# Layer norm of block 1 from the column copy of x, in a kernel of attention and a gated feed-forward

## The chip, the cores and the metric

The kernel runs on one core of a Trainium2 chip. The core has a matrix engine (TensorE, PE in the profile; PEld is its loading of weights), a vector engine (VectorE, DVE), a scalar engine (ScalarE, ACT), GpSimd (POOL) and SyncE (SP), which here only issues transfers. Each engine works off its own list of instructions in order. They meet through semaphores. Transfers between DRAM and the on-chip memory (SBUF) run on 16 DMA engines; SyncE, ScalarE and GpSimd each have a queue of them. Products come out in PSUM, a small memory of eight banks.

The metric is the device time of one execution in microseconds (us), as the median of several runs.

## What is computed

With x of 2048 rows and 512 columns, the reference is, cut to what matters:

```python
xn = _layernorm(x, axis=-1)          # (x - mean) / sqrt(var + 1e-5), row by row
s = _A_ref(xn, A_wqkv, A_wo)         # 32 heads of 16: softmax(q k^T / 4) v, then @ wo
g = _silu(_B_ref(xn, ...))           # (silu(xn @ w_gate) * (xn @ w_up)) @ w_down
return x + s * g
```

All inputs and the output are float32.

## The kernel before

**Blocks and slots.** The 2048 rows of x are four blocks of 512 (`TB`), each of four tiles of 128 rows. A prologue makes queries, keys and values of all blocks. For each block it makes twelve products: eight feature tiles (128 features of q or k by 512 rows) and four value tiles (128 rows by 512 values). Block 0 begins with its value tiles, the others end with them. The loop at the end of the prologue numbers these twelve by `n`; `12 * b + n` is called a slot here. After the prologue the attention and the feed-forward network run interleaved on TensorE; the change does not touch that part.

**Operands in two parts.** Products run in a reduced float32 format, and every operand is split in a high part and the remainder: x into `xt` (hi and lo, two sets, so that block b uses set b % 2), the weights into `wh` and `wl` (features) and `vh` and `vl` (values). A product over 512 inputs is 12 matrix instructions: for each of the four chunks c of 128 inputs hi by wh, lo by wh, hi by wl. So x must be normalised and lie transposed, inputs on partitions.

**Weights.** Twelve pieces of the weights are loaded on SyncE's queue some five slots ahead (`load_w`), cast on ScalarE two slots ahead (`high_w`), and subtracted on GpSimd (`low_w`, which needs the cast). Pieces 8 to 11 are the value weights, 0 to 7 the features in slots 4 to 11; "weight 4" is piece 4, used in slot 8.

**Two ways to a transposed x.** Blocks 0 and 1 load rows. VectorE makes mean and variance of each tile (`stats`), the rate 1 / sqrt(var + eps) of all (`rates`), and the normalised rows (`norm`); TensorE turns them in four 128 by 128 transposes per tile (`turn`), ScalarE copies the high part out of PSUM and VectorE subtracts the low part (`split_x`). Blocks 2 and 3 (`columns_of`) load rows only for the statistics and, beside them, x transposed from a second copy of the input (`A_x_columns`). Mean and rate of each row are then wanted along the free axis on all partitions. So `spread_mr` transposes the eight columns of means and rates on TensorE, copies them on ScalarE into `rows_mr`, and writes them to DRAM (`mr_d`, 4 KB) on ScalarE's queue. `load_mr` reads them back, broadcast to 128 partitions (`wide_mr`, 512 KB). Per chunk of columns VectorE then subtracts and multiplies in place, ScalarE casts the high part, VectorE makes the low part.

**The order.** It is written out by hand. `columns_of` puts its steps into a table by slot: `ats` gives, in this order, the slots of the rows' load, the columns' load, the first statistics, the rates, the spread (its read-back one slot later), and the first chunk, and then, for each chunk, how many slots after the first chunk's slot its low part is made. `step(at, 0, ...)` runs ahead of that slot's product, `step(at, 1, ...)` behind it. Block 1's own steps stand in the loop: `load_x(1)` at n = 2, statistics at 2 and 3, rates at 4, `norm` at 6 to 9, `turn_x` at 7 to 10. Its normalised x goes to DRAM for the feed-forward network (`store_x`, GpSimd's queue); block 0's is copied on chip by ScalarE, one piece per slot (`copy_fx`).

**What limits a slot.** A product's bank is one of four (`pps`). ScalarE squares it and casts it into `parts`, VectorE subtracts, and SyncE stores `parts` (512 KB) to `q_d` or `k_d`; there are four `parts` buffers. The load of block 0 and of each later block's rows goes into `xin`, which is the tile `facc`, or into `raw_x`.

## Time and profile before

| | |
|---|---|
| median of 3 runs | 1385.1 us (1385.07 to 1385.13) |
| the profiled execution | 1385.12 us |
| its span | 1383.3 us, 27675 instructions |
| granted TensorE clock | 1.00 of full speed |

The profile shows one execution. A row of a timeline is: start in us from the span's start, duration in us (of the whole group, where several instructions are merged), engine, line of the kernel, operation, what it writes and reads, shapes, how many; in brackets how long the engine had been idle and what ended that. ACTq and SPq are the issues of transfers. Matrix instructions overlap, so their starts tell the pace better than their durations. In a row of stretches each engine's busy time stands with the number of its instructions in brackets. In the list of waits a row gives who waited for whom, the total, how often, and the longest.

### The profile page before, as it was taken

The numbers are of one execution on the slowest core, as the hardware profiler recorded it, in microseconds if no ns is written. First come the engines' busy times: TensorE is split into PE (matmuls) and PEld (weight loads), VectorE is DVE, ScalarE is ACT, GpSimd is POOL, SyncE is SP. The second block draws the span as 40 slices with busy tenths as digits, with TensorE's granted clock in tenths as the row PEclk, the third lists the DMA queues.
The fourth block names the chain that finished last, engine by engine and source line by source line (L and its number), as shares of the span: only waits on it lengthen the run. The fifth ranks groups of instructions, "written<-read, shape, count | busy, mean of one in ns | idle before, by whom it ended". The sixth has DMA issues, their size and how long they took to land.

```text
span 1383.3 us, 27675 instructions
## 1 busy us (share of the span) xinstructions
PE 1377.5 (100%) x11167; PEld 868.4 (63%) x11167; DVE 775.9 (56%) x1250; ACT 1158.2 (84%) x1943; POOL 103.5 (7%) x145
## 2 busy tenths in 40 slices
PE   9999999999999999999999999999999999999998
PEld 7787666656655665565566555566566556655665
DVE  6655466365545663565465643655466545655656
ACT  6644589888888898899998988888888888899875
POOL 4200100000010000000110000000100000000142
PEclk9999999999999999999999999999999999999999
DMA  7989541134553511233724402356333312234752
GB/s 238 307 283 297 147 106 44 36 77 106 111 128 82 135 44 36 51 90 86 173 56 115 110 13 51 74 127 145 83 78 83 101 25 59 59 86 133 226 188 84
DMA packets 132260, 154.71 MB, mean 112 GB/s; under 512 B 13489, under 2 KB 83137, under 8 KB 131358
## 3 DMA queue, kind: packets, MB, share of 16 engines
q1 hardware_dynamic: 124782, 128.03, 36.1%
q0 software_dynamic: 6880, 24.32, 5.2%
q8 instruction: 89, 1.46, 0.5%
q10 hardware_dynamic: 464, 0.53, 0.1%
q14 instruction: 45, 0.37, 0.1%
HBM read 110.61 MB, written 40.12 MB: 109 GB/s over the span
## 4 chain that ended last, share of the span: by engine, by line
PE 89%; DVE 0%; DVEq 0%; issue 0%
PE acc L450 33%; PE bankx L244 29%; PE score L981 10%; PE single L981 8%; PE banky L244 7%; PE spare L981 1%; PE spare L1036 0%; PE banky L1036 0%; DVE y L1043 0%; PE score L1036 0%; PE single L1036 0%; DVE y L1049 0%; DVEq L1096 0%
## 5 line engine op out<-in xcount | busy, mean ns | idle before, releaser
L450 PE MATMUL acc<-pr,vst 128*17 128x512 f32 x4096 | 459.3, 593 | 0.0
L991 ACT ACTIVATE pr<-single 128x512 f32<-128x512 f32 x762 | 429.3, 604 | 17.2 <-PE single L981 0.5
L984 ACT ACTIVATE pr<-score 128x1024 f32<-128x1024 f32 x318 | 327.9, 1031 | 87.1 <-PE score L981 84.3
L450 PEld LDWEIGHTS acc<-pr,vst 128*17 128x17 f32 x4096 | 115.6, 97 | 279.5 <-issue 275.3
L244 PE MATMUL banky<-fx,guh 64*128 64x512 f32 x896 | 290.8, 392 | 0.0
L244 PE MATMUL bankx<-fx,guh 64*128 64x512 f32 x896 | 290.5, 391 | 0.1
L988 DVE COPY pr<-spare 128x512 f32<-128x512 f32 x194 | 134.1, 691 | 182.5 <-PE spare L981 169.6
L981 PE MATMUL score<-qst,kst 50*128 50x512 f32 x830 | 218.8, 418 | 0.0
L981 PE MATMUL single<-qst,kst 50*128 50x512 f32 x922 | 212.6, 398 | 0.0
L244 PE MATMUL banky<-wd,hh 64*128 64x512 f32 x672 | 196.0, 391 | 0.0
L244 PE MATMUL bankx<-wd,hh 64*128 64x512 f32 x672 | 195.9, 391 | 0.0
L1001 ACT ACTIVATE pr<-pr 128x512 f32<-128x512 f32 x354 | 193.3, 641 | 0.0
L244 PEld LDWEIGHTS bankx<-fx,guh 64*128 64x128 f32 x896 | 166.8, 186 | 21.4 <-DVE guh L205 0.6
L244 PE MATMUL bankx<-fx,gul 64*128 64x512 f32 x448 | 175.6, 392 | 0.0
L244 PE MATMUL banky<-fx,gul 64*128 64x512 f32 x448 | 175.5, 392 | 0.0
L981 PEld LDWEIGHTS score<-qst,kst 50*128 50x128 f32 x830 | 98.9, 184 | 112.9 <-ACT pr L991 69.2
L244 PEld LDWEIGHTS banky<-fx,guh 64*128 64x128 f32 x896 | 166.9, 186 | 1.1
L991 ACT ACTIVATE pr<-score 128x512 f32<-128x512 f32 x194 | 116.9, 603 | 35.5 <-PE spare L981 27.7
L988 DVE COPY pr<-single 128x512 f32<-128x512 f32 x160 | 110.5, 691 | 59.1 <-PE single L981 49.3
L244 PEld LDWEIGHTS bankx<-wd,hh 64*128 64x128 f32 x672 | 125.1, 186 | 17.8
L981 PEld LDWEIGHTS single<-qst,kst 50*128 50x128 f32 x922 | 114.8, 184 | 23.0 <-ACT pr L991 7.6
L244 PEld LDWEIGHTS banky<-wd,hh 64*128 64x128 f32 x672 | 125.1, 186 | 5.9
(191 smaller groups left out, 1689.9 us busy)
## 6 DMA issues: line engine op xcount, KB each, us to landing
gur<-in_B_w_gate_dram SPq DMA_DIRECT2D x56, 256.0 KB
gur<-in_B_w_up_dram SPq DMA_DIRECT2D x56, 256.0 KB
wdr<-in_B_w_down_dram SPq DMA_DIRECT2D x56, 256.0 KB
kst<-k_d SPq DMA_DIRECT2D x192, 64.0 KB
qst<-q_d SPq DMA_DIRECT2D x192, 64.0 KB
fx<-xt_d SPq DMA_DIRECT2D x24, 512.0 KB
q_d<-parts SPq DMA_DIRECT2D x16, 512.0 KB
k_d<-parts SPq DMA_DIRECT2D x16, 512.0 KB
```

The source lines that it names most:

```text
L244: mm(bank, lhs[h], rhs[h], start=start, stop=stop)
L450: mm(acc[h * 32:h * 32 + DH + 1], v[:, kt % CT, h * (DH + 1):(h + 1) * (DH + 1)], probs[2 * i + h // 2][:, h % 2], start=kt == 0, stop=kt ...
L981: mm(banked[h], k[r, j, kc * P:(kc + 1) * P], q[r, j], start=True, stop=True)
L984: exps.append(act(pr, both_banks, AF.Exp, scale=0.25))
L988: dve.tensor_copy(pr[:, h], banked[h])
L991: exps.append(act(pr[:, h], banked[h], AF.Exp, scale=0.25))
L1001: exps.append(act(part, part, AF.Exp, scale=0.25))
```

## The change

Block 1 now goes through `columns_of` too. Its call is `columns_of(1, raw_x, xin, (1, 2, 2, 3, 5, 7, (1, 1, 2, 3)))`: rows into `raw_x` at slot 1, columns into `xin` at slot 2, statistics at 2 and 3, rates behind slot 3's product, the spread ahead of slot 5's, the read-back behind the same product and on GpSimd's queue, the first chunk at slot 7 and one more per slot. The row loads, norms and transposes of block 1 go. The rates run before the first of block 0's copies for the feed-forward network, and those copies move one slot later. Block 2's rows are loaded at slot 9 instead of 7 and its columns at 14 instead of 12; its statistics move from 10 to 12, its rates from 12 to 14, its spread from 14 to 16, while its first chunk stays at 19. Block 3's rows move from 11 to 13 and its statistics from 15 to 17.

```diff
-        def load_x(b):
-            for t in range(NT):
-                load_tile(b * NT + t)
...
         def turn_x(b, t, between=None):
             split_x(b, t, turn(t), between)
-            if t == NT - 1 and b:
-                store_x(b)
...
         def load_mr(b):
-            sp.dma_start(wide_mr, mr_d[b].rearrange("s t p -> s (t p)")[None].to_broadcast([P, 2, TB]))
+            (pool if b == 1 else sp).dma_start(wide_mr, mr_d[b].rearrange("s t p -> s (t p)")[None].to_broadcast([P, 2, TB]))
...
-            step(rated, 0, rates_x)
+            step(rated, b == 1, rates_x)
             step(spread, 0, spread_mr, b)
-            step(spread + 1, 0, load_mr, b)
+            step(*((spread, 1) if b == 1 else (spread + 1, 0)), load_mr, b)
...
-        columns_of(2, raw_x, raw_x, (7, 12, 10, 12, 14, 19, (1, 2, 3, 3)))
-        columns_of(3, xin, raw_x, (11, 24, 15, 24, 26, 31, (1, 2, 3, 3)))
+        columns_of(1, raw_x, xin, (1, 2, 2, 3, 5, 7, (1, 1, 2, 3)))
+        columns_of(2, raw_x, raw_x, (9, 14, 12, 14, 16, 19, (1, 2, 3, 3)))
+        columns_of(3, xin, raw_x, (13, 24, 17, 24, 26, 31, (1, 2, 3, 3)))
...
-                if not b and n == 2:
-                    load_x(1)
...
-                if not b and 6 <= n < 10:
-                    norm(n - 6)
...
-                if b < 2 and 0 <= 12 * b + n - 3 < 16:
-                    copy_fx(12 * b + n - 3)
+                if b < 2 and 0 <= 12 * b + n - 4 < 16:
+                    copy_fx(12 * b + n - 4)
...
-                if not b:
-                    for t in range(NT):
-                        if n == 2 + t // 2:
-                            stats(t)
-                    if n == 4:
-                        rates(0, NT)
-                    if 7 <= n < 11:
-                        turn_x(1, n - 7)
```

Three places show how the instructions move. The first is GpSimd's list from the low part of weight 2 to the store of block 1's x. Before:

```order
L578 TENSOR_TENSOR wl<-wraw,wh 128x512 [waits DMAHW3_49,Activation_49]
L578 TENSOR_TENSOR wl<-wraw,wh 128x512 [waits DMAHW4_49,Activation_49]
L578 TENSOR_TENSOR wl<-wraw,wh 128x512 [waits DMAHW1_49,Activation_49]
L578 TENSOR_TENSOR wl<-wraw,wh 128x512 [waits DMAHW2_49,Activation_49]
L578 TENSOR_TENSOR wl<-wraw,wh 128x512 [waits DMAHW4_49,Activation_49]
L578 TENSOR_TENSOR wl<-wraw,wh 128x512 [waits DMAHW6_49,Activation_49]
L664 DMA xt_d<-xt_171 128x2048 [waits Activation_49]
```

After, the same stretch:

```order
L574 TENSOR_TENSOR wl<-wraw,wh 128x512 [waits DMAHW3_49,Activation_49]
L574 TENSOR_TENSOR wl<-wraw,wh 128x512 [waits DMAHW5_49,Activation_49]
L679 DMA wide_mr<-mr_d 128x1024 [waits DMAHW2_49]
L574 TENSOR_TENSOR wl<-wraw,wh 128x512 [waits DMAHW7_49,Activation_49]
L574 TENSOR_TENSOR wl<-wraw,wh 128x512 [waits DMAHW0_49,Activation_49]
L574 TENSOR_TENSOR wl<-wraw,wh 128x512 [waits DMAHW3_49,Activation_49]
L574 TENSOR_TENSOR wl<-wraw,wh 128x512 [waits DMAHW5_49,Activation_49]
L658 DMA xt_d<-xt_171 128x2048 [waits Activation_49]
```

The read of the broadcast rates stands between the low parts of weights 3 and 4 and waits for the write of `mr_d`.

The second is VectorE's list from slot 5's eviction to just behind slot 9's (`parts` is an eviction; `xt_172` is the low part of block 1's x). Before:

```order
L772 TENSOR_TENSOR parts<-ps,parts 128x512 [waits Activation_49]
L638 TENSOR_SCALAR xn<-facc,mv,mr 128x512 [waits DVE_49]
L772 TENSOR_TENSOR parts<-ps,parts 128x512 [waits Activation_49]
L638 TENSOR_SCALAR xn<-facc,mv,mr 128x512
L772 TENSOR_TENSOR parts<-ps,parts 128x512 [waits Activation_49]
L655 TENSOR_TENSOR xt_172<-acc,xt_171 128x4x128 [waits Activation_49]
L638 TENSOR_SCALAR xn<-facc,mv,mr 128x512 [waits DVE_49]
L772 TENSOR_TENSOR parts<-ps,parts 128x512 [waits DMAHW3_49,Activation_49]
L655 TENSOR_TENSOR xt_172<-extra,xt_171 128x4x128 [waits Activation_49]
L638 TENSOR_SCALAR xn<-facc,mv,mr 128x512 [waits DVE_49]
L772 TENSOR_TENSOR parts<-ps,parts 128x512 [waits DMAHW5_49,Activation_49]
L655 TENSOR_TENSOR xt_172<-acc,xt_171 128x4x128 [waits Activation_49]
```

After, from the evictions of slots 4, 5 and 6, which follow one another, to slot 9's:

```order
L766 TENSOR_TENSOR parts<-ps,parts 128x512 [waits Activation_49] x3
L667 TENSOR_TENSOR facc<-facc,wide_mr 128x512 [waits DMAHW6_49,DMASW2_49]
L667 TENSOR_TENSOR facc<-facc,wide_mr 128x512 [waits DVE_49]
L766 TENSOR_TENSOR parts<-ps,parts 128x512 [waits Activation_49]
L667 TENSOR_TENSOR facc<-facc,wide_mr 128x512
L667 TENSOR_TENSOR facc<-facc,wide_mr 128x512 [waits DVE_49]
L766 TENSOR_TENSOR parts<-ps,parts 128x512 [waits DMAHW1_49,Activation_49]
L667 TENSOR_TENSOR xt_172<-facc,xt_171 128x512
L667 TENSOR_TENSOR xt_172<-facc,xt_171 128x512 [waits Activation_49]
L667 TENSOR_TENSOR facc<-facc,wide_mr 128x512
L667 TENSOR_TENSOR facc<-facc,wide_mr 128x512 [waits DVE_49]
L766 TENSOR_TENSOR parts<-ps,parts 128x512 [waits DMAHW4_49,Activation_49]
```

Where a norm and a low part stood between two evictions, two operations on columns and a low part stand now, and the first of them waits for the read on GpSimd's queue (DMASW2).

The third is ScalarE's list from slot 4's eviction to slot 5's (`top` is the square, `fx` the copy for the feed-forward network). Before:

```order
L770 ACTIVATE top_156<-ps 128x512 [waits PE_49]
L771 CAST parts<-ps 128x512
L811 COPY fx<-xt_169 64x2x512
L624 ACTIVATE nw<-mv,root 128x4 [waits DVE_49]
L574 CAST wh<-wraw 128x512 [waits DMAHW4_49]
L770 ACTIVATE top_157<-ps 128x512 [waits PE_49]
```

After:

```order
L764 ACTIVATE top_156<-ps 128x512 [waits PE_49]
L765 CAST parts<-ps 128x512
L805 COPY fx<-xt_169 64x2x512 [waits Activation_49]
L570 CAST wh<-wraw 128x512 [waits DMAHW5_49]
L675 COPY busy<-extra 8x128 [waits DMASW0_49,PE_49]
L676 DMA mr_d<-busy 8x128 [waits Activation_49]
L764 ACTIVATE top_157<-ps 128x512 [waits PE_49]
```

The square root for the rates has left this place (it runs ahead of weight 2's cast), and the copy and the write of the rates (`busy` is `rows_mr`) stand behind the cast of weight 3.

## The prediction

> **What bounds the kernel now.** I read the page's head, then the chain of work that ended last, then the timeline of the first 80 us engine by engine, because the change touches nothing later.

> ```profile
> span 1383.3 us, 27675 instructions
> ...
> PE 1377.5 (100%) x11167; PEld 868.4 (63%) x11167; DVE 775.9 (56%) x1250; ACT 1158.2 (84%) x1943; POOL 103.5 (7%) x145
> ...
> PE 89%; DVE 0%; DVEq 0%; issue 0%
> ```

> TensorE is busy for 1377.5 of 1383.3 us, and the chain is TensorE's own order and almost nothing else. So work taken off TensorE in the first 45 us shortens the span by its issue time, and a wait put on TensorE there lengthens it by as much. All other engines count only where TensorE comes to wait for them.

> I call the twelve products of a block slots: 0 to 3 are block 0's value tiles, 4 to 11 its feature tiles, 12 the first tile of block 1, 24 the first of block 2.

> ```profile
> 31.81 0.60 PE L643 MATMUL acc<-ident,xn 128*128 128x128 f32 x4
> 32.16 0.70 PE L718 MATMUL ps<-xt,wh 128*128 128x512 f32 x2
> 32.70 0.40 PE L718 MATMUL ps<-xt,wl 128*128 128x512 f32 x1
> 32.94 0.63 PE L718 MATMUL ps<-xt,wh 128*128 128x512 f32 x2
> 33.40 0.39 PE L718 MATMUL ps<-xt,wl 128*128 128x512 f32 x1
> 33.63 0.63 PE L718 MATMUL ps<-xt,wh 128*128 128x512 f32 x2
> ...
> 44.71 1.00 PE L718 MATMUL ps<-xt,wh 128*128 128x512 f32 x2
> 45.55 0.39 PE L718 MATMUL ps<-xt,wl 128*128 128x512 f32 x1
> ...
> 50.68 0.27 PE L680 MATMUL extra<-ident,mr 128*8 128x128 f32 x1
> 50.71 0.71 PE L718 MATMUL ps<-xt,wh 128*128 128x512 f32 x2
> 51.25 0.40 PE L718 MATMUL ps<-xt,wl 128*128 128x512 f32 x1
> ```

> Starts are what counts. Three products take 33.63 - 32.94 = 0.69 us, a slot of twelve 2.8, and a pair 0.46. From 31.81 to 32.70 four transposes and a pair take 0.89, so four transposes cost 0.43.

> **What leaves TensorE's path.** Slots 8 to 11 each lose four transposes: 4 x 0.43 = 1.72. At 44.71 the pair takes 0.84 instead of 0.46: TensorE waits 0.38 for the last tile of block 1, which was turned only at the end of slot 11. That wait goes if the columns are ready in time. Added is one transpose of the rates at slot 5: 51.25 - 50.68 = 0.57 for it and a pair, so 0.11. Together 1.72 + 0.38 - 0.11 = 1.99, about 2.0 us. This is the most that the change can bring, and block 1 would begin at 44.71 - 1.72 + 0.11 = 43.1.

> The removed VectorE and ScalarE work (four norms, four copies and subtractions out of PSUM, four statistics) and the added (four subtractions, four multiplications, four low parts, four casts) lie beside TensorE. They cost nothing as long as block 1's twelve operands stand when TensorE reads them. The later place of the feed-forward copies (one slot) costs nothing either: they fill the same ScalarE time in each slot. The rows and columns are 2 MB on SyncE's queue ahead of weights 4 and 5, where 1 MB of rows stood. The transfers pause just behind them, as the first row below shows, so they have room for the extra 1 MB, and weight 3 is cast only at 25.71, 4 and 5 after it. I take zero there.

> ```profile
> 19.00:23.00 4.00, 4.00 (x19) 3.23 (x18) 3.71 (x9) 2.68 (x5) 2.27 (x3) 1.00 0.03 6
> 26.00:31.00 5.00, 5.00 (x23) 4.05 (x22) 3.40 (x10) 4.84 (x8) 2.60 (x2) 1.00 0.99 286
> 53.00:59.00 6.00, 6.00 (x28) 4.81 (x27) 2.58 (x7) 2.79 (x6) 0.00 (x0) 1.00 1.05 346
> 86.00:91.00 5.00, 5.00 (x23) 4.04 (x22) 1.79 (x4) 1.81 (x4) 0.00 (x0) 1.00 1.02 388
> ```

> These are stretches by engine; the last three columns are granted clock, DMA share and GB/s. The transfers are idle from 19 to 23 us (0.03) and full from 26 to 31 (0.99).

> **The new wait: rates out to DRAM and back.** Before, block 1's mean and rate were used where they were made. Now they go through a transpose, a ScalarE copy, a write (mr_d), and a broadcast read (wide_mr, 512 KB) before VectorE can start. In the new order ScalarE's copy stands behind the cast of weight 3.

> ```profile
> 25.51 0.30 ACT L624 ACTIVATE nw<-mv,root 128x4 f32<-128x4 f32 x1
> 25.71 0.61 ACT L574 CAST wh<-wraw 128x512 fp32r<-128x512 f32 x1
> ...
> 52.93 0.25 ACT L681 COPY busy<-extra 8x128 f32<-8x128 f32 x1
> 53.21 0.52 ACTq L682 DMA_DIRECT2D mr_d<-busy  x1
> ...
> 59.11 0.33 SPq L685 DMA_DIRECT2D wide_mr<-mr_d  x1
> ...
> 85.88 0.27 ACTq L682 DMA_DIRECT2D mr_d<-busy  x1
> ...
> 90.92 0.33 SPq L685 DMA_DIRECT2D wide_mr<-mr_d  x1
> ...
> SPq L685 <- DMA mr_d<-busy: 2.2, 1, 2.2
> ...
> 142.45 0.35 SPq L882 DMA_DIRECT2D s_d<-shift  x1
> ...
> 145.83 0.56 POOL L885 DMA_DIRECT2D sh_d<-s_d  x1 [31.31 <-DMA s_d<-shift]
> ```

> The square root moves away from 25.51, so the cast runs there, the copy from about 26.0, and the write starts at about 26.3. How long this write takes at that place no row shows. Blocks 2 and 3 wrote 4 KB from 53.21 to 59.1 (5.9 us; SyncE waited for it) and from 85.88 to 90.9 at most (5.0), both with full transfers; the small write at 142.45 took 3.4 at a slacker time. At 26.3 the transfers are full, but only for about three microseconds, since 23. I take 4.4, between the slack row and the nearer of the full ones: landed at 30.7, with ends 29.7 and 32.2.

> GpSimd waits for it in its own queue, and behind it stands the low part of weight 4, which slot 8 reads at about 32.4 (31.81 + 0.11 and a pair). With the landing at 30.7, 0.56 for the issue and 1.30 for the low part (both in rows here), it is done at 32.6: late by 0.2, which the later wait swallows.

> The read is priced by what GpSimd's queue moved.

> ```profile
> v_d<-vt POOLq DMA_DIRECT2D x1, 1088.0 KB, 5.3
> sh_d<-busy POOLq DMA_DIRECT2D x1, 256.0 KB, 4.3
> ...
> xt_d<-xt POOLq DMA_DIRECT2D x4, 1024.0 KB, 11.4
> ...
> g_d<-y POOLq DMA_DIRECT2D x16, 256.0 KB, 2.7
> ```

> Last column: us from issue to landing. The first two are of the first 30 us and bracket 512 KB: 4.6. The ends are 4.3 and half of the crowded 11.4, 5.7. So VectorE can begin at W = 30.7 + 0.1 + 4.6 = 35.4, between 34.0 and 38.0. It is done with slot 6's eviction some 2 us after that slot's end at 29.1, so it stands there from about 31.

> [...]

> **What follows from W.** VectorE then works off block 1's columns between the evictions of slots 7 to 10.

> ```profile
> 71.88 1.41 DVE L673 TENSOR_TENSOR raw_x<-raw_x,wide_mr 128x512 f32<-128x512 f32 x2
> 73.21 0.68 DVE L772 TENSOR_TENSOR parts<-ps,parts 128x512 fp32r<-128x512 f32 x1
> 73.81 0.41 DVE L776 TENSOR_TENSOR top<-top,sq 128x512 bf16<-128x512 bf16 x1
> ...
> 79.34 1.46 DVE L673 TENSOR_TENSOR xt<-raw_x,xt 128x512 fp32r<-128x512 f32 x2
> ...
> 78.78 0.63 PE L718 MATMUL ps<-xt,wh 128*128 128x512 f32 x2
> ...
> 26.92 0.80 DVE L633 SCALAR_TENSOR_TENSOR mr<-nw,mr 128x4 f32<-128x4 f32 x1
> ...
> 48.88 0.16 DVE L633 SCALAR_TENSOR_TENSOR mr<-nw,mr 128x4 f32<-128x4 f32 x1
> ...
> 26.40 1.30 POOL L578 TENSOR_TENSOR wl<-wraw,wh 128x512 fp32r<-128x512 f32 x1 [2.17 <-ACT wh L574]
> ```

> Block 2's same chain ran from 71.88 to 80.80, 8.9 us with one eviction in it. Block 1's has four; three more at 0.60 (73.81 - 73.21) make 10.7. Then GpSimd: the four-element operation with two SBUF inputs took 0.80 instead of 0.16 and ended with GpSimd's low part (26.40 + 1.30 = 27.70). So VectorE operations with two SBUF inputs seem to be held while GpSimd runs one. The low parts of weights 6 and 7 fall into the chain; I take 0.8 for each, between nothing and 1.3. That gives 12.3, ends 10.7 and 13.3. ScalarE, which waits for the first column inside its own order and then has an eviction, a copy of 1.05 and a cast in each slot, would come to about the same.

> So the last low part stands at W + 12.3 = 47.7. TensorE needs it for the eleventh product of block 1, at 43.1 + 10 x 2.8 / 12 = 45.4. It waits 2.3 in all, part of it already in slots 10 and 11, where the cast of weights 6 and 7 stands behind ScalarE's wait. The sum is -2.0 + 2.3 = +0.3. In general the change is W - 35.1 for the middle chain, and never below -2.0.

> **Block 2** loses spare time too: its rates now leave at slot 16 and are needed at slot 19, three slots instead of five. In the rows above its last low part ends at 80.80 and is needed at 78.78 + 2.33 = 81.1, so 0.3 to spare. By the same ScalarE order the write leaves at about 58 and the read at about 63 on SyncE, some 4 us later than now (59.11). VectorE may start at 72.2 at the latest, so the read has 9 us. Before it had 12.8 and showed no wait. By the GpSimd rows 512 KB needs 4.3 to 5.7; I take no wait, end +2.5 if it needs all it may have used now.

> The profiled execution took 1385.12 (1383.3 of span and 1.8 around it), the median 1385.1. The sum against the first is 1385.12 + 0.3 = 1385.4.

> **The rivals.**
> - The gain stays whole. It needs W below 33.1. For it speaks the 256 KB row with 2.7: a write of 2.7 and a read of 2.7 + 0.8 for the further 256 KB (at about 320 GB/s) give W = 32.6. Against it stand the full transfers from 26 to 31. Time 1385.1 - 2.0 = 1383.1. [...]
> - The round trip is as slow as block 2's. The write takes 5.9 and the read 5.7: W = 38.0, and the change is +2.9, to +3.9 with the full hold by GpSimd. Weight 4's low part is then at 32.2 + 0.1 + 0.56 + 1.30 = 34.2, and slot 8 already stands for 1.8 of it. Slower begins to be told from W = 37.9. Time 1388.0 to 1389.0.
> - Block 2's read is late behind the stores and loads on SyncE's queue, as worked out: with no loss in block 1 besides the sum, +0.3 + 2.5, 1387.9.
> - The rates don't reach the transposition at slot 5 in time, since VectorE's two-input operation falls beside weight 2's low part. At most 0.6, and it only moves part of the later wait forward. It decides nothing.

> **How the numbers follow.** A change of under 0.2%, 2.8 us, is about what a measurement of this kernel tells from none. The forecast (W between 34 and 37.9, change -1 to +2.7) has 0.50; the whole gain 0.20; the slow round trip 0.17; block 2's late read 0.08; something beyond 2.8 us of gain, say less crowding later, 0.05. The first two are both within 0.2%: 0.70. Slower: 0.17 + 0.08 = 0.25. The range reaches from the whole gain to the slow round trip, 1383.0 to 1388.9, and leaves out its far end and the gain that I cannot name.

> **What would show it.** Right: VectorE idle before its first column operation until 34 to 38 us, with a transfer as releaser; ScalarE idle before the first cast of a column; TensorE late by about 2 us between slots 10 and 12; from there all as before, shifted by less than 1 us. Wrong: a first column operation at about 31 (then -2), or waits of TensorE over 1 us before block 2 or in slot 8.

## The result and the profile after

| | before | after |
|---|---|---|
| median, lowest to highest (6 runs each) | 1385.11 us (1384.84 to 1385.18) | 1392.16 us (1390.94 to 1392.93) |
| the profiled execution | 1385.12 us | 1392.93 us |
| its span, mean granted clock | 1383.3 us, 1.000 | 1391.1 us, 0.997 |

The ratio is 1.005, with a 95% interval of 1.0039 to 1.0061. The kernel is slower by 7.05 us in the median and by 7.8 us in the profiled executions. The forecast was 1385.4 and the range ended at 1388.9, so both are missed.

These rows of the page of the kernel after answer to those shown of before: the span, the engines' busy time, the transfers of code (pieces, MB, share), and the scores' matrix instructions (busy us, mean ns, idle before and its releaser). The last row is from the list of transfers: the broadcast read on GpSimd's queue.

```profile
span 1391.1 us, 27653 instructions
PE 1379.8 (99%) x11152; PEld 869.8 (63%) x11152; DVE 778.6 (56%) x1255; ACT 1157.6 (83%) x1944; POOL 104.5 (8%) x146
q8 instruction: 90, 1.47, 0.5%
L964 PE MATMUL score<-qst,kst 50*128 50x512 f32 x830 | 219.1, 418 | 2.2 <-issue 2.2
wide_mr<-mr_d POOLq DMA_DIRECT2D x1, 512.0 KB, 6.1
```

The page of before has for code and scores:

```profile
q8 instruction: 89, 1.46, 0.5%
L981 PE MATMUL score<-qst,kst 50*128 50x512 f32 x830 | 218.8, 418 | 0.0
```

TensorE has 15 matrix instructions fewer and still 2.3 us more busy time, which points to a lower clock somewhere; the rest of the 7.8 are waits. To place them, take the start of each slot's first product in both profiles, and count from the start of slot 4 (20.61 in before, 20.50 in after), so that the few tenths in which the beginnings differ drop out:

| shift against before, us | slot 12 | slot 14 | slot 24 | slot 25 | slot 47 | end of the span |
|---|---|---|---|---|---|---|
| after | +2.94 | +2.51 | +2.47 | +3.90 | +4.00 | +7.9 |

Three losses stand out: one before slot 12, one at slot 24, and 3.9 us somewhere behind the prologue, in the part that the change does not touch.

**The first loss, at block 1.** The timeline of after, from the transposition of the rates in slot 5 to the first product of block 1:

```profile
23.92 0.27 PE L674 MATMUL extra<-ident,mr 128*8 128x128 f32 x1 [0.46 <-DVE mr L629]
26.21 0.52 ACTq L676 DMA_DIRECT2D mr_d<-busy  x1
30.11 0.57 POOL L679 DMA_DIRECT2D wide_mr<-mr_d  x1 [2.72 <-DMA mr_d<-busy]
30.70 1.31 POOL L574 TENSOR_TENSOR wl<-wraw,wh 128x512 fp32r<-128x512 f32 x1
36.24 1.42 DVE L667 TENSOR_TENSOR facc<-facc,wide_mr 128x512 f32<-128x512 f32 x2 [4.56 <-DMA q_d<-parts]
37.69 0.62 ACT L667 CAST xt<-facc 128x512 fp32r<-128x512 f32 x1 [2.88 <-DVE facc L667]
38.22 0.61 ACT L570 CAST wh<-wraw 128x512 fp32r<-128x512 f32 x1
38.88 0.72 PE L712 MATMUL ps<-xt,wh 128*128 128x512 f32 x2 [0.69 <-ACT wh L570]
38.91 1.80 POOL L574 TENSOR_TENSOR wl<-wraw,wh 128x512 fp32r<-128x512 f32 x1 [4.87 <-ACT wh L570]
40.77 0.50 PE L712 MATMUL ps<-xt,wl 128*128 128x512 f32 x1 [1.16 <-POOL wl L574]
41.10 1.02 PE L712 MATMUL ps<-xt,wh 128*128 128x512 f32 x2
42.34 1.05 PE L712 MATMUL ps<-xt,wh 128*128 128x512 f32 x2
```

The write lands at about 30.1 (3.9 us), the read at 36.2 (6.1): VectorE's first column operation starts at W = 36.2. (The row names a store as what ended its wait; by the page's 6.1 us for the read it was the read, 30.1 + 6.1.) ScalarE waits 2.88 for its result, and only behind that wait stands the cast of weight 6 in its order (38.22). So TensorE waits 0.69 in slot 10 for the high part of the weight and, since GpSimd needs that cast, 1.16 more for the low part. Then two matrix instructions take 1.0 instead of 0.63. A row of stretches (after the engines' busy times stand the granted clock, the DMA share and GB/s) says why, here of after:

```profile
40.00:50.00 10.00, 9.23 (x33) 7.41 (x34) 9.19 (x13) 9.23 (x14) 3.51 (x5) 0.83 0.88 274
160.00:170.00 10.00, 9.80 (x67) 7.64 (x71) 1.53 (x3) 7.70 (x12) 3.78 (x4) 0.83 0.51 118
```

The granted clock is 0.83 of full speed over 10 us, worth 1.7 us, in two places: behind these waits, and at the start of the attention.

**The second, at block 2.** Its rates, and what becomes of them, in the timeline of after:

```profile
61.22 0.58 ACT L765 CAST parts<-ps 128x512 fp32r<-128x512 f32 x1 [1.68 <-DMA k_d<-parts]
...
62.93 0.27 ACTq L676 DMA_DIRECT2D mr_d<-busy  x1
67.98 0.33 SPq L679 DMA_DIRECT2D wide_mr<-mr_d  x1
75.84 1.42 DVE L667 TENSOR_TENSOR raw_x<-raw_x,wide_mr 128x512 f32<-128x512 f32 x2 [3.17 <-DMA wide_mr<-mr_d]
84.03 0.51 PE L712 MATMUL ps<-xt,wh 128*128 128x512 f32 x1 [0.97 <-DVE xt L667]
```

ScalarE waits for a store to free a `parts` buffer; behind that stand the copy and the write of the rates (62.93). The read is issued at 67.98 and takes 7.9. VectorE, ready 3.17 before, starts at 75.84, and TensorE waits 0.97 in slot 24 for the last low part.

**The third, at the first scores.** The timeline of after where TensorE passes from the prologue to the attention; line 964 makes the scores, and nothing of it was changed:

```profile
157.55 0.46 PE L964 MATMUL score<-qst,kst 50*128 50x512 f32 x1
...
160.20 0.46 PE L964 MATMUL score<-qst,kst 50*128 50x512 f32 x1 [2.19 <-issue]
160.75 1.02 ACT L967 ACTIVATE pr<-score 128x1024 f32<-128x1024 f32 x1 [3.30 <-DMA v_d<-vt]
160.91 1.00 PE L964 MATMUL single<-qst,kst 50*128 50x512 f32 x2
```

And before:

```profile
153.68 0.70 PE L981 MATMUL score<-qst,kst 50*128 50x512 f32 x2
```

Before, the two score products run together. After, the second comes 2.19 later, and the releaser is "issue": no semaphore held it. The half clock follows (1.00 for a pair). The store named behind the activation misleads: the activation starts at 160.75, just behind the end of the second score product (160.20 + 0.46).

No row names what TensorE waited for. Between the prologue and the attention the program has a branch: a general path for other masks (an If on line 873) whose code stands in TensorE's program and is jumped over here. The change took 30 instructions out of the code ahead of it (15 transposes less, each a weight load and a multiplication) and put 4 semaphore waits in: 26 in all (the trace has 1398 of TensorE's instructions ahead of the first score product in before and 1372 in after). The row q8 of the page counts 90 pieces with 1.47 MB of code, 16.3 KB each; before has 89. In the trace of after each piece has 16384 bytes, and TensorE passes 256.0 of its instructions per piece (1640 ahead of the piece that starts at 177.02, 22119 ahead of the one at 1357.83, 80 pieces later; 256.0 in before too). Behind the branch TensorE goes through 16 instructions from 156.87 on and then stands, and a piece is under way from 157.16 to 158.62. The author's theory was that TensorE waits for this piece, so that the place of the code decides it. Experiments 1 and 2 test this.

### The profile page after: what moved, and what is told of

It reads as the page before. It is cut to its first block, busy times and chain, and to the rows that moved or that the text cites. A ratio compares the mean times of both kernels' runs of the same rounds, so it can differ in the third digit from the quotient of the medians.

```text
span 1391.1 us, 27653 instructions
## 1 busy us (share of the span) xinstructions
PE 1379.8 (99%) x11152; PEld 869.8 (63%) x11152; DVE 778.6 (56%) x1255; ACT 1157.6 (83%) x1944; POOL 104.5 (8%) x146
## 3 DMA queue, kind: packets, MB, share of 16 engines
q1 hardware_dynamic: 125262, 129.08, 36.2%
q8 instruction: 90, 1.47, 0.5%
## 4 chain that ended last, share of the span: by engine, by line
PE 88%; issue 0%; DVE 0%; DVEq 0%
PE acc L450 33%; PE bankx L244 30%; PE score L964 10%; PE single L964 8%; PE banky L244 6%; PE spare L964 1%; PE spare L1019 0%; PE banky L1019 0%; PE single L1019 0%; DVE y L1026 0%; PE score L1019 0%; DVE y L1032 0%; DVEq L1079 0%
## 5 line engine op out<-in xcount | busy, mean ns | idle before, releaser
L974 ACT ACTIVATE pr<-score 128x512 f32<-128x512 f32 x194 | 117.1, 603 | 35.5 <-PE spare L964 26.6
L964 PEld LDWEIGHTS single<-qst,kst 50*128 50x128 f32 x922 | 115.2, 185 | 23.2 <-ACT pr L974 7.3
## 6 DMA issues: line engine op xcount, KB each, us to landing
gur<-in_B_w_gate_dram SPq DMA_DIRECT2D x56, 256.0 KB
gur<-in_B_w_up_dram SPq DMA_DIRECT2D x56, 256.0 KB
wdr<-in_B_w_down_dram SPq DMA_DIRECT2D x56, 256.0 KB
```

What stands on the lines that cost most here:

```text
L964: mm(banked[h], k[r, j, kc * P:(kc + 1) * P], q[r, j], start=True, stop=True)
L974: exps.append(act(pr[:, h], banked[h], AF.Exp, scale=0.25))
```

## The experiments

All medians stand beside the kernel before run on the same chip (medians of 1385.04 to 1385.13; experiments 5 to 8 had another chip than the rest). The ratio is to it, with its 95% interval. The last column is the forecast made for the run; only experiments 6, 12 and 13 came within it.

| | kernel | median, us (range; runs) | ratio | forecast, us |
|---|---|---|---|---|
| | after | 1392.16 (1390.94 to 1392.93; 6) | 1.005 (1.0039 to 1.0061) | |
| 1 | after, 26 instructions that never run | 1389.52 (1388.77 to 1390.91; 6) | 1.0034 (1.0022 to 1.0047) | 1388.2 (1387.6 to 1388.8) |
| 2 | before, 230 instructions that never run | 1387.80 (1386.76 to 1389.60; 10) | 1.0022 (1.0012 to 1.0031) | 1388.4 to 1389.6 |
| 3 | 1, casts of weights 6 and 7 earlier | 1389.03 (1388.12 to 1389.88; 8) | 1.0028 (1.0018 to 1.0039) | 1386.2 (1385.4 to 1387.2) |
| 4 | 1, block 1 without the round trip | 1386.39 (1386.01 to 1386.72; 10) | 1.0009 (1.0000 to 1.0019) | 1385.2 (1384.4 to 1386.2) |
| 5 | 1, block 2's rates earlier | 1388.17 (1387.29 to 1388.88; 9) | 1.0021 (1.0011 to 1.0032) | 1387.4 (1386.9 to 1388.0) |
| 6 | 3 and 5 together | 1387.06 (1386.45 to 1388.48; 10) | 1.0016 (1.0006 to 1.0026) | 1387.4 (1386.6 to 1388.6) |
| 7 | 4 and 5 together | 1384.74 (1384.45 to 1385.03; 10) | 0.9998 (0.9988 to 1.0007) | 1384.2 (1383.6 to 1384.7) |
| 8 | before, blocks 2 and 3 at the new times | 1385.36 (1384.78 to 1386.32; 10) | 1.0003 (0.9993 to 1.0012) | 1387.3 (1386.4 to 1387.8) |
| 9 | 6, GpSimd's low part held back | 1387.43 (1385.71 to 1390.51; 10) | 1.0018 (1.0008 to 1.0027) | 1386.5 (1386.2 to 1386.8) |
| 10 | 9, rates written without transposition | 1410.96 (1410.30 to 1411.94; 4) | 1.0185 (1.0168 to 1.0202) | 1384.4 (1383.9 to 1385.0) |
| 11 | 9, rates written sooner | 1385.02 (1384.28 to 1386.82; 10) | 1.0001 (0.9991 to 1.0011) | 1385.9 (1385.3 to 1386.5) |
| 12 | 6, the read on SyncE's queue | 1386.59 (1386.12 to 1387.33; 10) | 1.0012 (1.0002 to 1.0022) | 1387.1 (1386.5 to 1387.7) |
| 13 | 11, the read on SyncE's queue, ahead of a store | 1384.38 (1383.48 to 1384.59; 11) | 0.9994 (0.9985 to 1.0003) | 1384.4 (1383.9 to 1384.9) |

### 1 and 2: code that never runs

Experiment 1 puts 13 transposes (26 instructions) into the path that is jumped over, and so restores the distance from there on. Experiment 2 puts 115 (230 instructions, 26 fewer than the 256 of a piece) into before. By the count in the forecasts the code behind stands one instruction further still, 27 and 231.

```diff
             with tc.tile_pool(name="gen", bufs=1) as gen:
+                unrun = pps.tile([P, 512], F32, tag="ps", name="ps")
+                for _ in range(13):      # 115 in before
+                    nc.tensor.transpose(unrun[:, :P], ident, ident)
```

> The changed kernel with 13 transposes added to the general branch of the If, which is not taken here: no executed instruction, wait or transfer differs, only the place of TensorE's later code (27 instructions further; the change had moved it 26 nearer). Theory of the code's place: the 2.2 us in which TensorE waits for nothing at the second score product (160.20 in the changed kernel) is a fetch of its next block of code, which a branch leaves too little time for when the block ends some 15 instructions behind the branch's target; with the place restored the wait goes, and with it the half clock behind it (1.00 for pairs up to 163.90): 3.9 us less, 1388.2 (1387.6 to 1388.8). Rival, the start of attention waits for data (the late store of the value tiles, which the profile names as releaser of the first exponential, or loads on queues whose numbering shifted): nothing changes, 1392.1 (1391 to 1393).

> The kernel before with 115 transposes added to the branch that is not taken: its executed program is the same, but TensorE's code behind the If stands 231 instructions further, that is 25 nearer to the start of a block if code comes in blocks of 256 instructions. Theory of the code's place: the wait of the changed kernel at its second score product appears here too, 2 to 3 us plus up to 1.7 us of half clock: 1388.4 to 1389.6, and nothing before the If moves. Rival, the wait comes from what the change did to transfers: no difference, 1385.1 (1384.8 to 1385.4).

The first scores in the timeline of experiment 1:

```profile
157.61 0.77 PE L967 MATMUL score<-qst,kst 50*128 50x512 f32 x2
```

and of experiment 2:

```profile
155.78 0.39 PE L984 MATMUL score<-qst,kst 50*128 50x512 f32 x1 [2.16 <-issue]
```

The wait is gone in the one (-2.64 in the median) and has come into the other (+2.7), without a single executed instruction being different. That the place of the code does it is shown. That the late thing is a piece of code fits the traces. Row q8 counts 90 pieces in after, and 89 in before and in experiments 6, 9 and 13, which do not wait there. In after one piece of 16384 bytes is under way from 157.16 to 158.62, and TensorE's next instruction starts at 159.99. The wait falls behind the first score product in after and just ahead of it in experiment 2 (155.78). That one instruction is the difference between 26 nearer and 25 (256 - 231), at 256 instructions to a piece. By the same count, as an estimate, a piece ends 16 instructions behind 156.87 in after and 10 ahead of the same place in before (16 - 26). Before fetches a piece there too (from 152.77 to 153.69), but does not come to wait for it: its first score product starts at 153.68 and the second runs with it.

Both amounts are smaller than the 4 us of after's profile, since the half clock behind the wait is not in every run. In experiment 2's own profile the clock stays full behind its 2.16 us (0.999 in the mean); of after's six runs three have a mean clock of 0.997 (1392.5 to 1392.9) and three 0.999 (1390.9 to 1391.8). All further experiments on the new kernel carry such code too (16 transposes in experiment 10, 13 in the others).

### 3: the casts of weights 6 and 7 a slot earlier

They now stand ahead of ScalarE's wait for the first column.

```diff
-                    if n >= 2 and n + 2 < 12:
-                        high_w(worder[n + 2])
-                        low_w(worder[n + 2])
+                    for m in range(n + 2 + (n > 7), min(n + 3 + (n >= 7), 12)) if n >= 2 else ():
+                        high_w(worder[m])
+                        low_w(worder[m])
```

> The changed kernel with the pad of the first run, and ScalarE's casts of weights 6 and 7 one slot earlier (in slots 7 and 8, ahead of its wait for block 1's first column); nothing else moves. Theory: the two waits of TensorE in slot 10 (0.83 and 1.43 us over the normal pace) and the half clock behind them (1.65) are caused by these casts standing behind ScalarE's 2.88 us wait. They go, 3.9 us; but then TensorE is early at block 1, whose last low part (48.7 at the earliest, since VectorE's chain starts at 36.2) holds it for about 1.9. Net -2.0 against the first run: 1386.2 (1385.4 to 1387.2). Rival: the wait only moves, since the last low part bounds block 1 in any case and the slow clock returns: within 0.5 us of the first run, 1388.2. Second rival: nothing waits at block 1 either, since the chain is shortened with ScalarE's: the whole 3.9, 1384.3.

The two waits in slot 10 are gone, and slot 12 begins 0.72 earlier than in before. There TensorE waits for block 1 itself, as its timeline shows:

```profile
47.48 0.50 PE L712 MATMUL ps<-xt,wh 128*128 128x512 f32 x1 [1.24 <-ACT xt L667]
...
49.91 1.05 PE L712 MATMUL ps<-xt,wh 128*128 128x512 f32 x2
```

The half clock came too (a pair takes 1.05; the granted clock is 0.95 from 40 to 50 us and 0.88 from 50 to 60). The median fell by 0.49 only. But slot 25 begins 64.88 behind slot 4 in after, 64.87 in experiment 1 and 64.58 here, whatever was lost before: block 2's broadcast sets that time. So this run could not show what the casts are worth; experiment 6 does.

### 4: block 1 without the round trip

```diff
-            (pool if b == 1 else sp).dma_start(wide_mr, mr_d[b].rearrange("s t p -> s (t p)")[None].to_broadcast([P, 2, TB]))
+            src = wqkv[:2, :TB] if b == 1 else mr_d[b].rearrange("s t p -> s (t p)")
+            (pool if b == 1 else sp).dma_start(wide_mr, src[None].to_broadcast([P, 2, TB]))
...
-            step(*((spread, 1) if b == 1 else (spread + 1, 0)), load_mr, b)
+            step(*((spread - 3, 1) if b == 1 else (spread + 1, 0)), load_mr, b)
```

> The changed kernel with the pad of the first run, where the broadcast for block 1 reads two rows of the weight matrix at the end of slot 2 in place of the rates at the end of slot 5: it leaves out that block 1 is normalised by its own mean and rate, and all instructions stay. This takes the round trip away and asks what the change brings without it. Theory: VectorE can start block 1's columns when it is free of slot 6, near 31; slot 10's waits and the slow clock go, no wait comes at block 1. Block 1 then begins at about 43.7 (the gain of 2.0 less the 0.6 at slot 5), against 45.1 before; block 2's 1.5 for its late read stays: 1385.1 - 1.4 + 1.5 = 1385.2 (1384.4 to 1386.2). Rival, the work of the columns itself is too much for VectorE and ScalarE beside slots 7 to 11, whatever the round trip: over 1387.2, and waits of over 1 us in slots 10 to 12 again.

This kernel leaves out block 1's own mean and rate: two rows of a weight matrix stand in their place. All waits between slots 8 and 13 are gone; block 1 stands 1.27 earlier than in before (slot 14) in spite of the wait of 0.44 in slot 5. 3.1 us come back against experiment 1. What is left is block 2: TensorE waits 0.20 and 0.96 in slot 24, and from slot 25 on the kernel is 0.8 late.

### 5: block 2's rates a slot earlier

```diff
-        columns_of(2, raw_x, raw_x, (9, 14, 12, 14, 16, 19, (1, 2, 3, 3)))
+        columns_of(2, raw_x, raw_x, (9, 14, 12, 13, 15, 19, (1, 2, 3, 3)))
```

> The kernel of the first run (1389.5) with block 2's rates, their transposition, write and broadcast read one slot earlier (rates at slot 13, spread at 15, read at 16). In the first run TensorE stood 2.1 us behind the kernel before at the start of block 2 and 3.9 one slot later, and so it did after the third run, which was 3.0 behind at that point: the broadcast of block 2 sets that time, whatever was lost before. Theory: with 2.8 us more for it the waits at slot 24 (0.20 and 0.97 over the pace and those between) go, and the shift stays at what block 1 lost: 1385.1 + 2.1 to 2.4 = 1387.4 (1386.9 to 1388.0). Rival, the last low part is held by VectorE's own work, not by the read: 1389.5, with the waits as before.

The write leaves at 59.12 instead of 63.23 and the read at 64.81 instead of 68.17; TensorE no longer waits for block 2. But the read takes 9.5 instead of 7.7, and VectorE starts only 1.6 sooner (74.28 against 75.86). The median falls by 1.35. A new wait of 0.50 stands at the transposition in slot 15.

### 6 and 7: block 2 out of the way

Experiment 6 has the edits of 3 and 5, experiment 7 those of 4 and 5 (its casts stay where after has them).

> The third run's kernel (casts of weights 6 and 7 a slot earlier, 1389.0) with block 2's broadcast one slot earlier as in the run before this one. Theory: the casts only move block 1's wait from slot 10 to slot 12, where the first column's high part and the last low part are late, and the clock falls to half behind the one or the other: within 0.8 us of the run before this one, 1387.4 (1386.6 to 1388.6). Rival: block 2 alone hid what the casts bring, and without it they bring the 1 to 2 us that slot 10 lost: 1385.8 or less.

> The fourth run's kernel (block 1 normalised by two rows of the weight matrix read at the end of slot 2, which leaves out its own mean and rate; 1386.4) with block 2's broadcast one slot earlier. Without either late read all that stays of the change is what TensorE no longer does: 16 transpositions less one and the wait at block 1, 2.0 us, less the 0.5 at slot 5. At slot 24 the fourth run stood 0.9 ahead of the kernel before. Theory: 1385.1 - 0.9 = 1384.2 (1383.6 to 1384.7), faster than the kernel before by little. Rival: another wait appears at blocks 2 or 3, since the stores of block 1 and block 2's loads stand later in the queues: 1385.0 or more.

TensorE's waits in block 1, timeline of experiment 6:

```profile
47.20 0.50 PE L712 MATMUL ps<-xt,wh 128*128 128x512 f32 x1 [0.93 <-ACT xt L667]
47.93 0.50 PE L712 MATMUL ps<-xt,wh 128*128 128x512 f32 x1 [0.22 <-DVE xt L667]
```

With block 2 out of the way the casts are worth 1.11 (1388.17 to 1387.06). The traces show where this comes from. Here are the third pair of column operations and GpSimd's low part of weight 7 in experiment 5, with TensorE's last wait in block 1, and then the same pair in experiment 6:

```profile
42.92 1.29 POOL L574 TENSOR_TENSOR wl<-wraw,wh 128x512 fp32r<-128x512 f32 x1 [1.40 <-ACT wh L570]
42.96 2.52 DVE L667 TENSOR_TENSOR facc<-facc,wide_mr 128x512 f32<-128x512 f32 x2
...
49.62 0.50 PE L712 MATMUL ps<-xt,wh 128*128 128x512 f32 x1 [0.22 <-DVE xt L667]
```

```profile
42.38 1.41 DVE L667 TENSOR_TENSOR facc<-facc,wide_mr 128x512 f32<-128x512 f32 x2
```

The late cast puts GpSimd's subtraction beside VectorE's columns, and the pair takes 2.52 instead of 1.41. Experiment 1 has the same 2.52. Its VectorE starts as far behind slot 4 as that of experiment 6 (15.58 and 15.56), both with a full clock, and slot 14 stands at +1.42 in the one and +0.29 in the other: 1.13. The waits in slot 10 are not lost on top: behind them TensorE still comes to wait for the last low part.

The round trip, with all that hangs on it, is worth 2.32 (1387.06 to 1384.74). Experiment 7 is 0.38 below the kernel before.

### 8: only block 2's and 3's times, in the kernel before

```diff
-        columns_of(2, raw_x, raw_x, (7, 12, 10, 12, 14, 19, (1, 2, 3, 3)))
-        columns_of(3, xin, raw_x, (11, 24, 15, 24, 26, 31, (1, 2, 3, 3)))
+        columns_of(2, raw_x, raw_x, (9, 14, 12, 14, 16, 19, (1, 2, 3, 3)))
+        columns_of(3, xin, raw_x, (13, 24, 17, 24, 26, 31, (1, 2, 3, 3)))
```

> The kernel before with only the times of blocks 2 and 3 of the changed kernel (rows of block 2 at slot 9, rates at 14, spread at 16, read at 17; block 3's rows at 13, counted at 17): the one part of the change done alone. Block 1 still comes from its rows, and the code's place is the old one. Theory: the broadcast's late read alone makes TensorE wait at block 2's last low part. In the fourth run the rates were turned at 54.9 and slot 25 began at 82.5, 27.6 later; here slot 16 begins at 56.4, so slot 25 at 84.0 in place of 81.8: 1385.1 + 2.2 = 1387.3 (1386.4 to 1387.8). Rival: the read is late only since block 1's columns and stores crowd ScalarE and the queues: 1385.1 to 1385.6.

```profile
59.82 0.52 ACTq L682 DMA_DIRECT2D mr_d<-busy  x1
64.06 0.33 SPq L685 DMA_DIRECT2D wide_mr<-mr_d  x1
71.81 0.69 DVE L673 TENSOR_TENSOR raw_x<-raw_x,wide_mr 128x512 f32<-128x512 f32 x1 [3.27 <-DMA wide_mr<-mr_d]
```

The rows are of its timeline. The read takes 7.7 us and VectorE starts at 71.81, just in time: nothing is lost (+0.24, not told from no change). The theory that the late times alone cost about 2 us fell. They use up the spare time, and the rest comes with block 1. Counted back from the start of slot 24, VectorE starts 6.63 ahead here, which is just enough, 5.31 ahead in after and 4.98 in experiment 4, where block 1 is on time. The 1.3 to 1.6 is spread: the write leaves 0.4 to 0.8 later, SyncE has the read out 0.6 to 0.8 later behind it (4.2 us here, 4.8 and 5.1 there), and the read takes 0.1 to 0.3 longer. That block 1's columns and stores crowd the transfers there is the reading that fits; no run separates these three.

### 9: GpSimd's low part behind the rates

GpSimd's subtraction for weight 2 is made to wait until VectorE has the rates, which it otherwise overlaps.

```diff
+                        part = low_w(worder[m])
+                        if m == 6:
+                            tc.add_manual_dep(part.ins, rated[0].ins.name, settled, reason="GpSimd would hold VectorE up")
```

> The sixth run's kernel (casts earlier, block 2 earlier, 1387.1) with one order added: GpSimd's low part of weight 2 starts only when VectorE has block 1's rates. In the runs so far the four-element operation that ends the rates took 1.02 us and ended with that low part, and TensorE waited 0.5 for it at slot 5. Theory: VectorE's operation with two SBUF inputs is held for as long as GpSimd runs one; then it takes 0.16 here, as it does for blocks 2 and 3, the 0.5 goes, and what follows from the rates comes 0.5 earlier: 1386.5 (1386.2 to 1386.8). Rival: the operation is slow for another reason, and the low part now comes late as well: 1387.1 to 1387.6.

The last operation of the rates in after, beside GpSimd's, and then the same in experiment 9 with the write that follows:

```profile
22.54 1.30 POOL L574 TENSOR_TENSOR wl<-wraw,wh 128x512 fp32r<-128x512 f32 x1
...
22.86 1.01 DVE L629 SCALAR_TENSOR_TENSOR mr<-nw,mr 128x4 f32<-128x4 f32 x1
```

```profile
23.24 0.16 DVE L629 SCALAR_TENSOR_TENSOR mr<-nw,mr 128x4 f32<-128x4 f32 x1
...
26.59 0.52 ACTq L679 DMA_DIRECT2D mr_d<-busy  x1
```

The operation takes 0.16 instead of 1.01 and TensorE's wait in slot 5 is gone. But the write leaves at 26.59, exactly as in experiment 6 (26.58): it stands behind a copy and a cast in ScalarE's order, and that sets its time. The median did not fall (+0.37 against experiment 6, ranges overlap). The hold is real; to end it here brought nothing that these runs can tell.

### 10: the rates written without transposition

SyncE writes the 1024 means and rates of each of the blocks 1 to 3 straight from where VectorE made them, four bytes each, block 1's one slot sooner. The transposition and ScalarE's copy go.

```diff
         def spread_mr(b):
...
+            sp.dma_start(mr_d[b].rearrange("s t p -> p s t"), mr)
```

> The run before this one, with the rates of all three blocks written to DRAM by SyncE straight from VectorE's result, 1024 pieces of 4 bytes, in place of the transposition, ScalarE's copy and ScalarE's write (8 rows of 512 bytes). Nothing is left out. Block 1's write would start at about 23.2 in place of 26.6. Theory: the broadcast's arrival decides, at 36.2 to 37.0 so far; if the write of small pieces takes the 3.9 us of the others it lands at 27.4 and the broadcast 6.7 later, at 34.1; the wait at block 1 falls from 2.3 to 1.0, the waits of 0.5 at slots 5 and 15 and three transpositions go: 1384.4 (1383.9 to 1385.0). Rival: 1024 small pieces take 6 us or more where 64 KB rows do not, the broadcast comes at 36.2 as before, and only the waits for the transpositions are saved: 1385.8 to 1386.6.

```profile
23.19 0.37 SPq L677 DMA_DIRECT2D mr_d<-mr  x1
37.88 0.57 POOL L680 DMA_DIRECT2D wide_mr<-mr_d  x1 [10.34 <-DMA mr_d<-mr]
```

The timeline shows the write under way from 23.19 to 37.88, 14.7 us instead of 3.9, with everything behind it on SyncE's and GpSimd's queues. TensorE waits 7.36 in slot 8 for a weight and 5.14 in slot 22 for a bank. The kernel is 25.9 us slower than before.

### 11: the rates written sooner

ScalarE's copy and the write of block 1's rates go ahead of slot 4's copy for the feed-forward network.

```diff
-            step(spread, 0, spread_mr, b)
+            step(*((spread - 1, 2) if b == 1 else (spread, 0)), spread_mr, b)
...
+                run_steps(12 * b + n, 2)
                 if b < 2 and 0 <= 12 * b + n - 4 < 16:
```

> The ninth run's kernel (casts earlier, block 2 earlier, GpSimd's low part after the rates, 1387.4) with ScalarE's copy of block 1's rates and its write ahead of slot 4's copy for the feed-forward and weight 3's cast instead of behind them: the write would start at about 25.1 in place of 26.6, everything else stays. Theory, the arrival W of the broadcast sets block 1's end and the time follows it one to one: W comes 1.5 earlier than 37.1, at 35.6, and the time 1.5 less than 1387.4: 1385.9 (1385.3 to 1386.5). Rival: an earlier write only meets the transfers that fill the engines then, so the broadcast arrives at 36.5 to 37 in any case: 1387.0 to 1387.6.

```profile
24.38 0.52 ACTq L679 DMA_DIRECT2D mr_d<-busy  x1
27.82 0.57 POOL L682 DMA_DIRECT2D wide_mr<-mr_d  x1
34.21 1.42 DVE L668 TENSOR_TENSOR facc<-facc,wide_mr 128x512 f32<-128x512 f32 x2 [3.58 <-DMA wide_mr<-mr_d]
```

Counted from slot 4, the timeline has W 1.51 earlier than in experiment 6 (14.05 against 15.56), and slot 14 is 1.51 earlier too (-1.22 against +0.29). One to one. Experiments 1 and 5 say the same: W is 1.22 later in the one profile than in the other, and so is slot 14. The median is 2.4 below experiment 9, more than the 1.5 expected.

### 12 and 13: the read on SyncE's queue

In 12 the read stands on SyncE's queue at slot 6. In 13, on top of 11, it stands there at slot 5, ahead of a store and of weight 7's load.

```diff
-            (pool if b == 1 else sp).dma_start(wide_mr, ...)
+            sp.dma_start(wide_mr, ...)
...
-            step(*((spread, 1) if b == 1 else (spread + 1, 0)), load_mr, b)
+            step(spread + 1, 0, load_mr, b)            # experiment 12
+            step(spread + (b > 1), 0, load_mr, b)      # experiment 13
```

> The sixth run's kernel (casts earlier, block 2 earlier, 1387.1) with block 1's broadcast read on SyncE's queue at the start of slot 6, as for blocks 2 and 3, in place of GpSimd's: this undoes one part of the change alone. GpSimd then doesn't wait for the write ahead of weight 4's low part. Theory: the read takes as long on either queue, since the 16 engines carry both; SyncE reaches it at 30.2 behind the load of weight 7, and q's store behind it comes later by little: within 0.6 of the sixth run, 1387.1 (1386.5 to 1387.7). Rival, SyncE's queue holds it behind a store and a load as it held block 2's read (7.9 us): VectorE starts at 38.1 in place of 36.5 and the time is 1388.7. Second rival, this queue is faster: the read takes 4 us, VectorE starts at 34.6 and the time is 1385.4.

> The eleventh run's kernel (1385.0, beside 1385.1 of the kernel before) with block 1's broadcast read on SyncE's queue at slot 5, ahead of the store of query tile 1 and the load of weight 7, in place of GpSimd's queue. Theory, the time follows the broadcast's arrival W one to one: if the read goes ahead of these 768 KB, W comes 0.5 to 1.5 before the eleventh run's (14.05 us after slot 4's start), and the time falls by as much until the wait at block 1, 0.9 there, is gone: 1384.4 (1383.9 to 1384.9), below the kernel before. Rival: the store and the weight behind the read come late in turn and TensorE or ScalarE wait for them, or the read is as slow on this queue: 1385.0 to 1386.

First 12, then 13, from their timelines:

```profile
29.80 0.96 SPq L679 DMA_DIRECT2D wide_mr<-mr_d  x1
35.97 0.69 DVE L667 TENSOR_TENSOR facc<-facc,wide_mr 128x512 f32<-128x512 f32 x1 [4.38 <-DMA wide_mr<-mr_d]
```

```profile
27.12 0.34 SPq L682 DMA_DIRECT2D wide_mr<-mr_d  x1
32.12 2.39 DVE L668 TENSOR_TENSOR facc<-facc,wide_mr 128x512 f32<-128x512 f32 x2 [1.05 <-DMA wide_mr<-mr_d]
...
53.03 0.27 PE L677 MATMUL extra<-ident,mr 128*8 128x128 f32 x1 [1.51 <-DVE mr L629]
```

The queue alone changes nothing: in 12 VectorE starts 15.55 behind slot 4, in 6 it was 15.56. What counts is the transfer ahead of which the read is put: in 13 it takes 5.0 instead of 6.2 and begins sooner. Block 1 then has no wait at all, and slot 14 begins 2.11 earlier than in before. 1.51 is lost again at block 2's transposition in slot 15, for which VectorE makes the rates too late. The median is 0.66 below the 1385.04 of before beside it, and the runs do not overlap (1383.48 to 1384.59 against 1384.79 to 1385.39). This is under the 0.2% that the prediction takes as the limit, and the interval of the ratio reaches over 1: it is the best of the kernels here, by an amount that is hardly more than nothing.

## Why the prediction was wrong

Two steps failed: that the change touches nothing behind the first 80 us, and that TensorE does not wait for block 2. Besides, the read was priced too low, and the clock had no term. In medians the 7.05 us come apart as follows, with 95% intervals from resampling the runs. The order in which the edits were taken matters: the casts alone, with block 2 still late, are worth 0.49.

| part | us | interval | from |
|---|---|---|---|
| place of the code behind the branch | 2.64 | 1.0 to 3.5 | after to 1 |
| block 2's broadcast late | 1.35 | 0.6 to 2.7 | 1 to 5 |
| casts of weights 6 and 7 behind ScalarE's wait | 1.11 | 0.0 to 1.9 | 5 to 6 |
| block 1's round trip | 2.32 | 1.7 to 3.0 | 6 to 7 |
| what is left: the gain of 2.11, less 0.69 over slot 5 and 0.65 over slot 15 (waits of 0.43 and 0.54), less 0.39 unplaced | -0.38 | -0.6 to -0.2 | 7 to before |

The intervals are wide because kernels with the same steps up to there do not get the rates back at the same time: W, counted from slot 4, is 15.58 in experiment 1, 15.74 in after and 16.80 in experiment 5. What makes the read take 5.4, 6.1 or 7.0 there, no run shows.

**"The change touches nothing later": failed, by the largest single amount.** The first 80 us were all that the prediction looked at. The change shifts the code behind the branch by 26 instructions, and that costs 2.64. Without it after would stand at 1389.5, 0.6 above the range.

**Block 2, "I take no wait": failed.** Named as a rival (+2.5, chance 0.08), it happened with 1.35, net of the 0.6 that experiment 5 loses in slot 15. The +2.5 does not follow from the prediction's own figures: a read of 12.8 from 63 ends 3.6 behind the latest time of 72.2. The read was taken at 4.3 to 5.7, from rows of the first 30 us and of GpSimd's queue; on SyncE's queue at 68 it took 7.9. And its issue was forecast at about 63, "by the same ScalarE order", with no delay to that order from block 1; it came at 67.98, of which 2.3 is the shift of the slots themselves. Experiment 8 shows that without block 1's part no time is lost: write 59.82 (58 was forecast), read 64.06 (63), VectorE at 71.81 (72.2 was the latest). There too the read took 7.7; the spare time covered it. With these two failures out of the way, experiment 5 stands at 1388.2, inside the range.

**The gain of 2.0: right.** In experiment 13, where nothing waits ahead of slot 14, it begins 2.11 earlier than in before.

**The write at 4.4 and W = 35.4: right within their ends, but the read was priced too low.** The write took 3.9. The read took 6.1 where 4.6 was forecast, above the end of 5.7, and W came at 36.2, within 34.0 to 38.0. Weight 4's low part was done at 32.0 and slot 8 did not wait; 32.6 was forecast. The rival with the whole gain needed W below 33.1 and fell.

**The chain of 12.3, "W - 35.1" and "part of it already in slots 10 and 11": right.** The chain took 12.5 in after (36.24 to 48.74) and in experiments 1 and 5, with one hold by GpSimd of 1.1 where the prediction had two of 0.8, and 11.4 in experiment 6 without it (36.46 to 47.87). With W put in, at the time that it has in before's count, the formula gives +1.1 for experiment 1 and +2.3 for 5; slot 14 stands at +1.42 and +2.64. That experiment 6 stands at +0.29 where the sum had +0.3 is luck: its W is 0.8 later than forecast and its chain 0.9 shorter. So is the round trip's 2.32 beside the forecast wait of 2.3.

**The clock had no term.** In after the formula gives +1.2, and slot 14 stands at +2.51. Most of the difference is the half clock from 41.13 to 44.54, behind the waits in slot 10; experiments 1 and 5 had these waits with a full clock, and lie 0.3 above the formula.

**Slot 5's rates, "it decides nothing": right on the time, as experiment 9 shows,** since ScalarE's order sets when the write leaves, and the wait in slot 5 is swallowed by the later one. In experiment 7, which has no later one in block 1, it does count, with 0.69 (0.6 at most was forecast).

The chance for slower, 0.25, was too low mainly because the failures add up, while the rivals were weighed as if only one could happen.

## What to carry to other kernels

- Here the place of the code behind a branch counted: a wait with "issue" as its releaser, at code that the change does not touch, is tested by adding instructions that never run. 26 of them were worth 2.64 us, 0.19% (after to experiment 1).
- Where an engine gets a new wait, list everything behind it in that engine's order, and see what else moves with it. Here TensorE's waits for the late weights were swallowed by a later wait; what counted was GpSimd's work, which came to lie beside VectorE's (a pair of column operations took 2.52 instead of 1.41).
- A round trip through DRAM is priced from rows of the same stretch and the same queue. Here its issue ahead of a store and a load brought the read from 6.2 to 5.0 us (experiments 12 and 13); another queue alone did not move it (VectorE's start 15.55 and 15.56 behind slot 4, experiments 12 and 6).

## What the runs showed of the hardware

```profile
40.00:50.00 10.00, 9.12 (x38) 7.02 (x39) 9.20 (x13) 9.20 (x15) 3.51 (x5) 1.00 0.88 272
```

- A VectorE operation of four elements with two inputs from SBUF took 1.01 us beside GpSimd's subtraction (after) and 0.16 without it (experiment 9); a pair of 128x512 operations took 2.52 beside it and 1.41 without (experiments 5 and 6).
- A write of 4 KB took 3.9 us in 512-byte rows (after) and 14.7 us in 4-byte pieces (experiment 10). A broadcast read of 512 KB took between 5.0 us (experiment 13, block 1) and 9.5 (experiment 5, block 2).
